# Giving a four-row mask matmul all 128 rows of the array

One small matmul of a fused kernel adds a mask. Its two operands used four partitions; after the change they use all 128, with zeros in the added rows of one of them. Nothing else is altered.

## Chip, cores and metric

The kernel runs on one core of a Trainium2 chip. The metric is device time in microseconds of one execution; a profiled execution also gives the span from the first to the last instruction, which is about 1.7 us shorter. TensorE, VectorE, ScalarE, GpSimd and SyncE are written PE, DVE, ACT, POOL and SP in the profile, and PEld is TensorE's weight load. Each run is called fast or slow by its time; only fast runs are compared.

## The reference, cut to what matters

Attention with chunk selection over 4 batches, 8 heads, 768 positions and 64 channels, followed by a gated MLP. For each query an upper bound is formed for each of 24 chunks of keys, chunks later than the query's own are masked, and the best six are attended to:

```python
ub = np.sum(np.maximum(q[:, :, :, None, :] * k_min[:, :, None, :, :],
                       q[:, :, :, None, :] * k_max[:, :, None, :, :]), axis=-1)
causal = pos[:, None] // chunk >= np.arange(nc)[None, :]
ub = np.where(causal, ub, -1000000000.0)
top_chunks = np.argsort(ub, axis=-1)[..., -top_k:]
# ... masked softmax of q k^T over the chosen chunks, times v ...
# ... then relu(x @ w_in), a norm, a spatial matmul, a gate, and @ w_out ...
```

## The kernel before

Heads are worked on in 16 pairs. Per pair the bounds of the query tiles 1 to 5 (128 queries each) are made in one PSUM bank: two matmuls for the bound itself and one that adds the chunk mask. The mask has rank four, because a tile of 128 queries holds four chunks: `sub_chunk` says to which of the four a query belongs, `later` which chunks are later than that one.

```python
P = 128; CHUNK = 32                       # CPT = P // CHUNK = 4, NCH = 24
sub_chunk = cp.tile([CPT, P], F16)
later = cp.tile([CPT, 2, 2 * NCH - CPT], F16)
# ... set once at the start, from the identity and by a select on GpSimd ...

def bounds(self):
    ub = self.ub = ps_tr.tile([P, 512], F32, tag="tr", name="ub")
    for qi in range(1, NQT):
        for m in range(2):                                     # L220
            mm(ub[:, (qi - 1) * W:qi * W], lhsT=self.rq[:, m, qi * P:(qi + 1) * P],
               rhs=self.km[:, m].rearrange("p h c -> p (h c)"), start=(m == 0), stop=False)
        mm(ub[:, (qi - 1) * W:qi * W], lhsT=sub_chunk,         # L222
           rhs=later[:, :, NCH - CPT * (qi + 1):2 * NCH - CPT * (qi + 1)],
           start=False, stop=True)
```

So there are 16 groups of five units, and a unit is bound, bound, mask: 80 mask matmuls of 48 columns. Around them stand the score matmuls, exponentials on ScalarE, value matmuls and, from about 59 us on, the MLP of the batch before. Loads of q, k, v and of the MLP's weights are issued from GpSimd. A scheduler orders each engine's instructions when the program is built.

The softmax here doesn't subtract the row's maximum and nothing guards it: scores larger than these inputs give would overflow.

Of the kernel before, what the change touches and what calls it, by code (L numbers as in the profile page):

```python
# [11 lines left out]
F16 = mybir.dt.float16  # L12
# [4 lines left out]
P = 128  # L17
CHUNK = 32
# [30 lines left out]
def kernel(  # L49
# [13 lines left out]
    NCH = S // CHUNK  # L63
# [8 lines left out]
    CPT = P // CHUNK  # L72
# [3 lines left out]
    cp = ctx.enter_context(tc.tile_pool(name="const", bufs=1))  # L76
# [29 lines left out]
    kh_ring = [[ring.tile([P, S], F16, name=f"kh{i}_{hi}") for hi in range(2)] for i in range(NB)]  # L106
    identity = cp.tile([P, P], F16)
    tri = cp.tile([P, P], F16)
    sub_chunk = cp.tile([CPT, P], F16)
    later = cp.tile([CPT, 2, 2 * NCH - CPT], F16)  # L110
    expand = cp.tile([D, S], F16)
    eps_t = cp.tile([P, 1], F32)

# [16 lines left out]
    def init_expand():  # L130

        nc.vector.tensor_scalar(expand.rearrange("d (c s) -> d c s", s=CHUNK),
                                in0=identity[0:D, 0:NCH].unsqueeze(2).to_broadcast([D, NCH, CHUNK]),
                                scalar1=NEG, scalar2=None, op0=Alu.mult)
        nc.vector.tensor_copy(sub_chunk.rearrange("d (c s) -> d c s", s=CHUNK),
                              identity[0:CPT, 0:CPT].unsqueeze(2).to_broadcast([CPT, CPT, CHUNK]))

    def init_masks():

# [315 lines left out]
    at(B0, init_ring, 0)  # L455
    at(B0, init_small)
    at(B0, init_expand)
    at(B0, init_masks)
    at(B0, load_k, 0, 0, 1)
# [105 lines left out]
```

## Time and profile before

| | before |
|---|---|
| time, median (4 runs) | 234.35 us (233.95 to 236.59) |
| span of the profiled run, mean granted clock | 231.2 us, 0.999 |
| unit of two bounds and a mask, start to start | 277 ns |
| group of five units, to the next matmul | about 1.38 us |

The first part of the page gives each engine's busy time, its share of the span and its instructions:

```profile
PE 207.5 (90%) x2022; PEld 126.8 (55%) x2022; DVE 154.1 (67%) x453; ACT 164.6 (71%) x335; POOL 79.9 (35%) x99
```

TensorE is the busiest. The table by windows says where; its columns are the window, then busy time and instruction count for TensorE, its weight loads, VectorE, ScalarE and GpSimd, then clock, DMA share and GB/s:

```profile
60.00:90.00 30.00, 27.99 (x293) 17.92 (x292) 26.51 (x73) 23.49 (x50) 16.20 (x17) 1.00 2.24 141
90.00:120.00 30.00, 29.40 (x283) 17.25 (x281) 23.60 (x73) 23.40 (x51) 7.94 (x8) 1.00 1.29 147
120.00:150.00 30.00, 29.45 (x294) 17.86 (x293) 21.67 (x62) 24.45 (x51) 5.87 (x6) 1.00 0.44 60
```

From 60 us on it is TensorE's program that sets the pace. Before that the chain of waits (the chain that ended last), cut to 20 to 62 us, by line, reads:

```profile
by line: ACT e L263 35.0%; PE ub L220 8.9%; PE ub L222 7.4%; PE sc L258 7.1%; issue 5.9%; PE acc L281 5.3%; POOL vt_81 L335 3.4%; PE trm L244 2.4%; PE kTp L169 2.4%; ACT km_86 L188 2.2%; POOL e L270 2.1%; ACT a_413 L249 1.9%; ACT a_543 L249
```

Exponentials lead there, and the bounds and masks (`ub`) follow with 16%.

Now the mask itself. The groups of instructions, split by shape, list the mask's matmul, the bounds' matmul and both weight loads (busy us, mean ns of one, idle before):

```profile
L222 PE MATMUL ub<-later,sub_chunk 4*128 4x48 f16 x80 | 15.4, 193 | 0.0
L220 PE MATMUL ub<-km_86,rq 128*128 128x48 f16 x80 | 9.3, 192 | 2.1 <-ACT km_86 L188 0.7 <-DVE rq L209 0.6 <-ACT rq L211 0.5
L220 PEld LDWEIGHTS <-rq 128*128 128x128 f16 x160 | 10.4, 97 | 7.3 <-issue 2.1 <-DVE rq L209 0.8 <-ACT rq L211 0.6
L222 PEld LDWEIGHTS <-sub_chunk 4*128 4x128 f16 x80 | 7.3, 91 | 3.3
```

By the means a mask costs the same as a bound, about 190 ns. That is a trap: the duration of a matmul says little here of how soon the next one starts (65-column value matmuls of 193 ns each start 31 ns apart, below). The spacing is in the timeline of TensorE (start us, us from the first start to the last end of the row, line, tile, count):

```profile
33.31 0.44 PE L281 MATMUL acc<-vt_80,e 128*128 128x65 f16 x9
33.59 0.18 PE L220 MATMUL ub<-km_87,rq 128*128 128x48 f16 x1
33.70 0.19 PE L222 MATMUL ub<-later,sub_chunk 4*128 4x48 f16 x1
33.83 0.22 PE L220 MATMUL ub<-km_87,rq 128*128 128x48 f16 x2
33.98 0.19 PE L222 MATMUL ub<-later,sub_chunk 4*128 4x48 f16 x1
34.10 0.22 PE L220 MATMUL ub<-km_87,rq 128*128 128x48 f16 x2
34.26 0.19 PE L222 MATMUL ub<-later,sub_chunk 4*128 4x48 f16 x1
...
34.81 0.19 PE L222 MATMUL ub<-later,sub_chunk 4*128 4x48 f16 x1
34.93 0.23 PE L169 MATMUL kTp<-identity,k 128*128 128x128 f16 x1
```

Masks start every 0.277 us. Single records show that a mask starts 115 ns after the bound ahead of it and the next matmul 124 ns after the mask, while two bounds stand 25 to 40 ns apart. Nine 65-column value matmuls fit into 0.44 us: less the duration of the last, 0.19 us, that leaves eight steps of 31 ns.

### The profile page before, as it was taken

The page shows a single profiled execution, that of the slowest core. Times are in us where ns is not written, and L with a number is a line of the kernel's source. Part 1 is how long each engine was busy: PE and PEld are TensorE (multiplying, and loading weights), DVE is VectorE, ACT ScalarE, POOL GpSimd, SP SyncE. Part 2 cuts the span into 40 slices and gives each one's busy share as a digit, 9 for nine tenths or more (in the row PEclk, how much of TensorE's full clock was granted, in tenths as well). Part 3 has the DMA queues.
Part 4 walks back from the last instruction along what each step waited for, and adds up shares of the span by engine and source line. Part 5 has one row for each costly group of instructions (what it writes and reads, how often), then busy time and mean ns, then how long its engine had stood idle before and what let it go on. Part 6 is the DMA issues. An engine that isn't in the chain of part 4 may idle for free.

```text
span 231.2 us, 5296 instructions
## 1 busy us (share of the span) xinstructions
PE 207.5 (90%) x2022; PEld 126.8 (55%) x2022; DVE 154.1 (67%) x453; ACT 164.6 (71%) x335; POOL 79.9 (35%) x99
## 2 busy tenths in 40 slices
PE   0279999898799989999999999999999999999990
PEld 0166677575466656556555555665555655544430
DVE  5347887787869899987567957573477355276610
ACT  2416797798778887679798976688898976476033
POOL 7991879860975153117011131111111111100000
PEclk9999999999999999999999999999999999999999
DMA  7999999999999999949991096427220325530376
GB/s 42 188 154 150 142 157 150 192 157 156 171 146 153 128 110 147 133 82 137 205 197 34 3 62 88 78 48 173 110 54 12 31 52 102 168 129 0 68 112 231
DMA packets 111273, 26.89 MB, mean 116 GB/s; under 512 B 105872, under 2 KB 107664, under 8 KB 111248
## 3 DMA queue, kind: packets, MB, share of 16 engines
q0 software_dynamic: 76512, 12.19, 84.8%
q1 hardware_dynamic: 34736, 14.36, 31.6%
q8 instruction: 16, 0.26, 0.5%
q14 instruction: 9, 0.07, 0.1%
HBM read 24.38 MB, written 6.29 MB: 133 GB/s over the span
## 4 chain that ended last, share of the span: by engine, by line
PE 60%; ACT 13%; DVE 9%; DMA 7%; POOL 6%; issue 3%; SPq 1%; ACTq 0%; POOLq 0%; DVEq 0%
PE mlp L380 30%; PE sc L258 9%; ACT e L263 8%; PE acc L281 6%; PE ub L220 4%; PE ub L222 4%; DMA k<-in_k_dram 3%; DVE vn L404 3%; DMA xT<-x_1868 3%; PE tr L244 2%; POOL qs_83 L330 2%; ACT o L429 1%; PE tr L204 1%; POOL k L321 1%; DVE kmm L177 1%
## 5 line engine op out<-in xcount | busy, mean ns | idle before, releaser
L263 ACT ACTIVATE e<-sc 128x512 f16<-128x512 f32 x192 | 97.9, 554 | 20.9 <-PE sc L258 17.7
L380 PE MATMUL mlp<-w_in_sb,xT 128*128 128x512 f16 x192 | 51.9, 379 | 0.5 <-DMA xT<-x_1868 0.5
L270 POOL TENSOR_SCALAR_AFFINE_SELECT e<-e 128x768 f16<-128x768 f16 x24 | 21.2, 883 | 89.1 <-ACT e L263 89.0
L281 PEld LDWEIGHTS <-e 128*128 128x128 f16 x672 | 30.8, 97 | 16.2 <-POOL e L270 2.0
L380 PE MATMUL mlp<-vn,wsT 128*128 128x512 f16 x144 | 39.1, 379 | 0.0
L419 DVE SCALAR_TENSOR_TENSOR g<-mlp,b_col,u 128x512 f16<-128x512 f32 x24 | 18.0, 748 | 13.3 <-PE mlp L380 12.0
L380 PE MATMUL mlp<-w_out_sb,gT 128*128 128x512 f16 x96 | 26.3, 379 | 0.1
L429 ACT COPY o<-mlp 128x512 f32<-128x512 f32 x24 | 14.2, 590 | 15.3 <-PE mlp L380 11.5
L380 PEld LDWEIGHTS <-xT 128*128 128x128 f16 x192 | 17.0, 98 | 14.5 <-DMA xT<-x_1868 1.0
L392 DVE BATCH_NORM_STATS2 stats<-vraw 128x6 f32<-128x512 f32 x24 | 16.6, 690 | 8.3 <-ACT vraw L390 8.1
L380 PEld LDWEIGHTS <-wsT 128*128 128x128 f16 x144 | 12.9, 98 | 10.2
L390 ACT ACTIVATE vraw<-mlp 128x512 f32<-128x512 f32 x24 | 14.4, 600 | 5.1 <-PE mlp L380 5.1
L412 ACT ACTIVATE u<-mlp 128x512 f16<-128x512 f32 x24 | 14.5, 605 | 2.6 <-PE mlp L380 2.5
L319 POOL DMA_DIRECT2D k<-in_k_dram x14 | 14.5, 1052 | 4.9 <-DMA k<-in_k_dram 2.3
L222 PE MATMUL ub<-later,sub_chunk 4*128 4x48 f16 x80 | 15.4, 193 | 0.0
L220 PEld LDWEIGHTS <-rq 128*128 128x128 f16 x160 | 10.4, 97 | 7.3 <-issue 2.1
L281 PE MATMUL acc<-vt_80,e 128*128 128x65 f16 x252 | 13.8, 193 | 0.5 <-DVE x_1440 L289 0.5
L404 DVE TENSOR_SCALAR vn<-vraw,mv,rstd 128x512 f16<-128x512 f32 x24 | 12.9, 596 | 0.6 <-ACT rstd L402 0.6
L380 PEld LDWEIGHTS <-gT 128*128 128x128 f16 x96 | 8.6, 98 | 7.8 <-DMA gT<-g 1.1
L281 PE MATMUL acc<-vt_81,e 128*128 128x65 f16 x252 | 12.8, 193 | 0.0
L288 DVE RECIPROCAL rec<-acc 128x6 f32<-128x6 f32 x32 | 6.0, 187 | 8.2 <-PE acc L281 8.0
L220 PE MATMUL ub<-km_86,rq 128*128 128x48 f16 x80 | 9.3, 192 | 2.1 <-ACT km_86 L188 0.7
(225 smaller groups left out, 387.3 us busy)
## 6 DMA issues: line engine op xcount, KB each, us to landing
out_dram<-o SPq DMA_DIRECT2D x24, 256.0 KB, 2.3
k<-in_k_dram POOLq DMA_DIRECT2D x14, 192.0 KB, 11.3
vt_80<-in_v_dram POOLq DMA_DIRECT2D x3, 384.0 KB, 9.2
qs_84<-in_q_dram POOLq DMA_DIRECT2D x6, 192.0 KB, 8.9
vt_81<-in_v_dram POOLq DMA_DIRECT2D x3, 384.0 KB, 10.6
ws_raw<-in_moe_w_spatial_dram POOLq DMA_DIRECT2D x6, 192.0 KB, 8.1
w_in_sb<-in_moe_w_in_dram POOLq DMA_DIRECT2D x8, 128.0 KB, 5.3
qs_85<-in_q_dram POOLq DMA_DIRECT2D x4, 192.0 KB, 8.5
```

Of the source, the lines that this page charges most:

```text
L220: mm(ub[:, (qi - 1) * W:qi * W], lhsT=self.rq[:, m, qi * P:(qi + 1) * P], rhs=self.km[:, m].rearrange("p h c -> p (h c)"), start=(m == 0), ...
L222: mm(ub[:, (qi - 1) * W:qi * W], lhsT=sub_chunk, rhs=later[:, :, NCH - CPT * (qi + 1):2 * NCH - CPT * (qi + 1)], start=False, stop=True)
L258: mm(sc[:, col:col + n], lhsT=self.kh[hi][:, t * P:(t + 1) * P], rhs=self.a[hi][:, q0:q0 + n], start=True, stop=not diag)
L263: nc.scalar.activation(out=self.e[hi][:, g * 512:g * 512 + width], in_=sc[:, 0:width], func=Act.Exp, scale=scale)
L270: nc.gpsimd.affine_select(out=blk, in_=blk, compare_op=Alu.is_ge, fill=0.0, base=0, channel_multiplier=-1, pattern=[[0, NQT], [1, P]])
L281: mm(self.av[:, qi, :], lhsT=self.e[hi][:, c:c + P], rhs=self.v[hi][:, t, 0:D + 1], start=first and n == 0, stop=last and n == len(blocks) ...
L319: nc.gpsimd.dma_start(out=t[:, :, :, 1 - hi, :].rearrange("p x t d -> p (x t) d"), in_=source(k, b, h, 2))
L380: mm(st[group][:, 0:cols], lhsT=lhsT, rhs=rhs, start=(j == 0), stop=(j == n - 1))
L392: nc.vector.bn_stats(stats, st["vraw"][:, ti, :])
L404: nc.vector.tensor_scalar(st["vn"][:, ti, :], in0=st["vraw"][:, ti, :], scalar1=st["mv"][:, ti, 0:1], scalar2=st["rstd"][:, ti, :], op0=Al ...
L419: nc.vector.scalar_tensor_tensor(g, in0=vs, scalar=b_col[:, ti:ti + 1], in1=st["u"][:, ti, :], op0=Alu.add, op1=Alu.mult)
L429: nc.scalar.copy(o_sb, o_ps)
```

## The change

The intent is that the mask runs in the same form of the array as everything around it. In the built program a four-row operand gets an array tile of 32 rows by 128 columns; a 128-row operand gets 128 by 128, as all other matmuls have.

```diff
-    sub_chunk = cp.tile([CPT, P], F16)
-    later = cp.tile([CPT, 2, 2 * NCH - CPT], F16)
+    sub_chunk = cp.tile([P, P], F16)
+    later = cp.tile([P, 2, 2 * NCH - CPT], F16)
 ...
         nc.vector.tensor_copy(sub_chunk.rearrange("d (c s) -> d c s", s=CHUNK),
-                              identity[0:CPT, 0:CPT].unsqueeze(2).to_broadcast([CPT, CPT, CHUNK]))
+                              identity[:, 0:CPT].unsqueeze(2).to_broadcast([P, CPT, CHUNK]))
```

The first four columns of the identity are zero below row 3, so the added rows of `sub_chunk` are zero; those of `later` hold finite values that meet these zeros. The order of instructions on every engine is the same before and after.

## The prediction

> **What bounds the kernel now.** Mean clock 0.999 (cores view). TensorE is busy 207.5 of 231.2 us (engine table); by windows, 28.0 of 30 us from 60 to 90, 29.4 from 90 to 120, 29.5 from 120 to 150, with VectorE and ScalarE at 22 to 27. From 20 to 60 us it is busy 36.4 of 40 by modelled ends, but the chain of waits passes through ScalarE (exponentials), the mask groups and VectorE in turn. Until 19.6 us the chain is loads of k; from 180 us dense 512-column matmuls.
>
> **What the change does to an instruction.** The built program gives the four-row mask operands an array tile of 32 rows; all other matmuls have 128. Start to start in the timeline, in 15 of 16 groups of five: bound to mask 115 ns, mask to next matmul 124 ns. A unit of two bounds and a mask takes 277 ns. Full-row neighbours are much closer: bound to bound 25 to 40 ns, the 65-column value matmuls about 31 ns. The mask's weight load takes 90 ns against 95 for full rows, its matmul 191 against 182 to 196: row count is not the cost, the two transitions are. [...] With full rows every operand has the same tile[...]: I estimate 85 to 105 ns a unit. The mask matmul's own duration will hardly change; its spacing will.
>
> **Sum.** 80 masks x (277 - 95) ns = about 14.5 us less TensorE time. Nothing moves: the order on TensorE, ScalarE and the DMA queues is the same. Added: the setup copy of sub_chunk on 128 partitions for 4 (0.51 us, same elements a row) and the fill and select of `later` on GpSimd (0.16 and 0.26 us, same elements a row). I expect the same within 0.1 us.
>
> **How much is on the critical path.**
> - First group (11.7 us): 0.9 us shorter, but the chain there is the load of k landing at 19.6 us. Worth 0.
> - Five groups from 20 to 60 us: 4.5 us shorter, all on the chain, but ScalarE is busy 33 of 40 us, so part turns into waits for exponentials. Worth about 2 us.
> - Ten groups from 60 to 176 us: 9 us shorter, TensorE-bound. VectorE (26.5 of 30 us from 60 to 90) and ScalarE come nearer to the limit. Worth about 6.5 us.
> - After 180 us: 0.
>
> Together 8.5 us: **226.1 us**, range 222.8 to 229.9. Faster by over 2%: 0.9; within 2%: 0.09; slower by over 2%: 0.01.
>
> **What will show it right or wrong.**
> - Timeline: bound to mask and mask to next 25 to 45 ns; five units in about 0.5 us instead of 1.39. Above 100 ns, the tile of 32 rows was not the cause.
> - Groups: mask loads and matmuls 128*128, mean near 95 and 185 ns. TensorE's busy sum falls by 8 to 14 us.
> - Chain of waits: mask and bound lines fall from 8% together to 2 or 3%; exponentials and VectorE gain. TensorE's waits for ScalarE and VectorE grow by several us, mostly from 20 to 60 us.
> - The tail from 180 us on keeps its length.
>
> **What would make it wrong.** Full-row masks may be slow for another reason (the two-piece access of `later`, 24 columns twice): the gain halves. The freed time may be lost to ScalarE and VectorE from 60 us on (gain 4 to 5 us). Or shorter mask groups may relieve the chain entirely (gain 12 us).

80 x (277 - 95) ns is about 14.5 us, of which 0 + 2 + 6.5 + 0 = 8.5 us were put on the critical path. The 95 ns is the estimate, the middle of 85 to 105 ns; three starts at the 25 to 40 ns measured between bounds make 75 to 120 ns.

## The result, and the profile after

| | before | after |
|---|---|---|
| time, median (4 runs each) | 234.35 us | 224.72 us (223.5 to 225.59) |
| ratio of fast runs | | 0.957 (95% interval 0.948 to 0.965) |
| span, clock of the profiled run | 231.2 us, 0.999 | 221.8 us, 0.989 |
| unit of two bounds and a mask | 277 ns | 75 ns |

A ratio is the mean time of one kernel's fast runs over that of the other's fast runs of the same rounds, so not quite the ratio of the medians, which are over all runs of a kernel.

Busy times of the page, and the three windows, in the same columns:

```profile
PE 194.7 (88%) x2022; PEld 118.6 (53%) x2022; DVE 153.0 (69%) x453; ACT 163.8 (74%) x335; POOL 80.3 (36%) x99
```

```profile
60.00:90.00 30.00, 28.15 (x326) 17.85 (x327) 27.88 (x85) 24.62 (x54) 16.31 (x17) 1.00 2.24 147
90.00:120.00 30.00, 28.30 (x292) 16.48 (x289) 23.82 (x67) 25.03 (x52) 7.86 (x8) 1.00 1.12 147
120.00:150.00 30.00, 29.68 (x329) 18.07 (x328) 22.60 (x72) 26.13 (x57) 6.28 (x7) 1.00 0.50 62
```

TensorE is still busy nearly all the time from 60 us on, but starts more instructions in each window (x326 for x293 in the first): the same program runs through it faster. TensorE's busy sum fell by 12.8 us (207.5 to 194.7), the span by 9.4, so its idle time grew by 3.4 us.

The timeline of the same group as above:

```profile
31.85 0.59 PE L281 MATMUL acc<-vt_80,e 128*128 128x65 f16 x14
32.28 0.18 PE L220 MATMUL ub<-km_87,rq 128*128 128x48 f16 x1
32.30 0.18 PE L222 MATMUL ub<-later,sub_chunk 128*128 128x48 f16 x1
32.33 0.21 PE L220 MATMUL ub<-km_87,rq 128*128 128x48 f16 x2
32.38 0.18 PE L222 MATMUL ub<-later,sub_chunk 128*128 128x48 f16 x1
...
32.60 0.18 PE L222 MATMUL ub<-later,sub_chunk 128*128 128x48 f16 x1
32.63 0.49 PE L169 MATMUL kTp<-identity,k 128*128 128x128 f16 x6
```

From the first mask's start to the fifth's it is 0.30 us for 1.11 us. Each of the three starts of a unit is now 25 ns from the next (about 40 ns in the two groups before 22.3 us, where the records of full clock begin). The groups by shape show the same matmul with almost the same duration (187 for 193 ns), as a busy time of 8.2 for 15.4 us only because busy time doesn't count overlap twice:

```profile
L222 PE MATMUL ub<-later,sub_chunk 128*128 128x48 f16 x80 | 8.2, 187 | 0.0
L222 PEld LDWEIGHTS <-sub_chunk 128*128 128x128 f16 x80 | 6.8, 99 | 0.0
```

The chain of waits from 20 to 62 us, by line:

```profile
by line: DMA kT<-k 23.4%; DMA k<-in_k_dram 17.4%; PE sc L258 5.9%; PE acc L281 5.2%; issue 5.2%; DVE kmm L177 4.3%; POOL vt_82 L335 3.5%; POOL vt_81 L335 3.4%; DVE kmm L181 2.6%; PE mlp L380 2.6%; PE tr L244 2.3%; DVE max_283 L232 2.2%; POO
```

Bounds and masks are nearly gone from it, but so are most exponentials. Loads and transposing copies of k have taken their place, which the prediction had not foreseen. Over the whole span the pieces of this chain on bounds and masks sum to 18.6 us before and 3.1 us after, those on DMA to 16.6 and 39.2 us. The chain that ends last differs between executions: in the traces of the two repeats of the changed kernel, exponentials keep 8.4 us of the chain between 20 and 62 us (14.7 us before). What all three share is DMA, 15.6 to 17.2 us in this stretch, where before had none.

Since the order is the same, the same matmul can be looked up in both traces. The 400th starts at 46.53 us before and 43.20 us after (3.33 us won), the 600th at 65.02 and 62.99 us (2.03 us), the 1800th at 188.97 and 179.79 us (9.18 us). So the gain shrinks by 1.3 us between 43 and 63 us, although two more groups in this stretch free about 1 us each, and it grows by 7.1 us after that.

### The profile page after: what moved, and what is told of

Its sections match the earlier page's. It is cut to its first block, busy times and chain, and to the rows that moved or that the text cites. A ratio compares the mean times of both kernels' runs of the same rounds, so it can differ in the third digit from the quotient of the medians.

```text
span 221.8 us, 5296 instructions
## 1 busy us (share of the span) xinstructions
PE 194.7 (88%) x2022; PEld 118.6 (53%) x2022; DVE 153.0 (69%) x453; ACT 163.8 (74%) x335; POOL 80.3 (36%) x99
## 4 chain that ended last, share of the span: by engine, by line
PE 44%; DMA 18%; DVE 17%; ACT 9%; POOL 7%; issue 3%; POOLq 0%; ACTq 0%; DVEq 0%; SPq 0%
PE mlp L380 27%; PE sc L258 7%; DMA k<-in_k_dram 7%; PE acc L281 5%; DMA kT<-k 4%; ACT e L263 4%; DMA gT<-g 3%; DVE kmm L177 3%; DMA xT<-x_1868 3%; DVE kmm L181 2%; ACT o L429 2%; PE tr L244 2%; POOL qs_83 L330 2%; DVE vn L404 1%; POOL k L321 1%
## 5 line engine op out<-in xcount | busy, mean ns | idle before, releaser
L419 DVE SCALAR_TENSOR_TENSOR g<-mlp,b_col,u 128x512 f16<-128x512 f32 x24 | 17.9, 748 | 12.8 <-PE mlp L380 11.5
L429 ACT COPY o<-mlp 128x512 f32<-128x512 f32 x24 | 14.1, 590 | 14.2 <-PE mlp L380 10.5
L392 DVE BATCH_NORM_STATS2 stats<-vraw 128x6 f32<-128x512 f32 x24 | 16.6, 691 | 8.2 <-ACT vraw L390 8.1
L380 PEld LDWEIGHTS <-wsT 128*128 128x128 f16 x144 | 12.9, 97 | 10.1
L319 POOL DMA_DIRECT2D k<-in_k_dram x14 | 14.5, 1051 | 4.2 <-DMA kT<-k 1.7
L261 PE MATMUL sc<-tri,identity 128*128 128x128 f16 x48 | 11.1, 232 | 0.0
L220 PEld LDWEIGHTS <-rq 128*128 128x128 f16 x160 | 8.4, 99 | 5.1 <-issue 2.1
L177 DVE TENSOR_REDUCE kmm<-kT 128x24 f16<-128x768 f16 x10 | 9.4, 941 | 2.2 <-DMA kT<-k 2.2
```

The lines of the kernel that those rows point to most:

```text
L177: nc.vector.tensor_reduce(self.kmm[:, 0, :], self.kT.rearrange("d (c ch) -> d c ch", ch=CHUNK), axis=AX.X, op=Alu.max)
L319: nc.gpsimd.dma_start(out=t[:, :, :, 1 - hi, :].rearrange("p x t d -> p (x t) d"), in_=source(k, b, h, 2))
L380: mm(st[group][:, 0:cols], lhsT=lhsT, rhs=rhs, start=(j == 0), stop=(j == n - 1))
L392: nc.vector.bn_stats(stats, st["vraw"][:, ti, :])
L419: nc.vector.scalar_tensor_tensor(g, in0=vs, scalar=b_col[:, ti:ti + 1], in1=st["u"][:, ti, :], op0=Alu.add, op1=Alu.mult)
L429: nc.scalar.copy(o_sb, o_ps)
```

## The experiments

### Is it rows, or the form of the array? 64 and 68 rows

The diff is the same for both, with R = 64 or R = 68. In the built program 64 rows get an array tile of 64 by 128 and 68 rows one of 128 by 128. The order on TensorE is that of before. Both results are correct.

```diff
-    sub_chunk = cp.tile([CPT, P], F16)
-    later = cp.tile([CPT, 2, 2 * NCH - CPT], F16)
+    sub_chunk = cp.tile([R, P], F16)
+    later = cp.tile([R, 2, 2 * NCH - CPT], F16)
-                              identity[0:CPT, 0:CPT].unsqueeze(2).to_broadcast([CPT, CPT, CHUNK]))
+                              identity[0:R, 0:CPT].unsqueeze(2).to_broadcast([R, CPT, CHUNK]))
```

> 64 rows instead of 4 in both operands of the mask; the built program gives them an array tile of 64 rows. Theory [...]: nothing is gained, because 64 is still not the 128 of the neighbours: bound to mask about 115 ns, mask to next about 124 ns, 234.5 us, ratio 1.00 +- 0.01. Rival (the cost falls with the share of rows filled): a gain between none and the whole, about 5 us. Correct result.

> 68 rows, 60 short of full; the built program gives them an array tile of 128 rows. Theory (tile, not rows): the whole gain comes, gaps of 25 to 40 ns, 224.7 us, ratio 0.957 +- 0.01, as with 128 rows. Rival (all rows must be filled): gaps above 100 ns and no gain, or about half the gain. Correct result.

Timeline of TensorE with 64 rows:

```profile
26.03 0.19 PE L222 MATMUL ub<-later,sub_chunk 64*128 64x48 f16 x1
26.16 0.22 PE L220 MATMUL ub<-km,rq 128*128 128x48 f16 x2
26.31 0.19 PE L222 MATMUL ub<-later,sub_chunk 64*128 64x48 f16 x1
```

and with 68 rows:

```profile
25.62 0.18 PE L222 MATMUL ub<-later,sub_chunk 68*128 68x48 f16 x1
25.64 0.21 PE L220 MATMUL ub<-km,rq 128*128 128x48 f16 x2
25.70 0.18 PE L222 MATMUL ub<-later,sub_chunk 68*128 68x48 f16 x1
```

With 64 rows the gaps are 115 and 126 ns and a unit takes 280 ns: 234.62 us, ratio 1.007 (1.002 to 1.011), no gain at all. With four rows more the gaps are 25 ns, a unit 75 ns: 224.53 us, ratio 0.961 (0.956 to 0.966), the whole gain. The cost doesn't follow the share of rows filled; it jumps where the tile changes from 64 to 128 rows. To fill all rows, as the change does, is not needed.

### Is a four-row matmul slow in itself? Masks together

The five masks of a group are moved behind its ten bounds, with four rows and with 128. Only the first matmul of the bank now has `start=True`. The order on the other engines stays the same (compared on a copy with 128 rows and unshifted line numbers).

```diff
             for qi in range(1, NQT):
                 for m in range(2):
-                    mm(..., lhsT=self.rq[...], rhs=self.km[...], start=(m == 0), stop=False)
-                mm(..., lhsT=sub_chunk, rhs=later[...], start=False, stop=True)
+                    mm(..., lhsT=self.rq[...], rhs=self.km[...], start=(qi == 1 and m == 0), stop=False)
+            for qi in range(1, NQT):
+                mm(..., lhsT=sub_chunk, rhs=later[...], start=False, stop=(qi == NQT - 1))
```

> Four rows as before, but the five masks of a group stand together after the ten bounds, so a group changes the tile twice instead of ten times. Theory ([...]a mask by itself costs nothing special): mask to mask 25 to 40 ns, one gap of 115 and one of 124 ns left; a group falls from 1385 to about 570 ns, eight tenths of the gain: 227 us, ratio 0.965. Rival (every four-row matmul or its weight load is slow in itself, for example because the load isn't pulled ahead): mask to mask stays at 115 to 124 ns, a group about 900 ns or more, at most half of the gain: 230 us or more. Correct result.

> The same order with all 128 rows: the control for the order. Theory: no tile change is left to save, so as the changed kernel, 224.7 us, ratio 0.957 +- 0.006; gaps 25 to 40 ns. Rival (the order itself helps or hurts): differs by over 1.5 us. Correct result.

The timeline with four rows shows one group:

```profile
25.55 0.41 PE L220 MATMUL ub<-km,rq 128*128 128x48 f16 x10
25.89 0.29 PE L223 MATMUL ub<-later,sub_chunk 4*128 4x48 f16 x5
26.12 0.51 PE L245 MATMUL trm<-identity,qs 128*128 128x128 f16 x6
```

Five four-row masks take 0.29 us from the first start to the last end; single records put them 25 to 40 ns apart, as close as full-row ones. Only the way in (115 ns) and the way out (110 ns) remain. Time: 226.23 us, ratio 0.970 (0.965 to 0.974), which by the medians is 7.1 of the 8.8 us that full rows gain in the same call, the eight tenths expected. With 128 rows in this order: 224.56 us, ratio 0.962 (0.958 to 0.966), the same as the change. So a four-row matmul among its like is not slow here; the change of the tile between two matmuls is, and it can also be made rarer by ordering.

### Which stage gives the gain? Full rows early or late only

Both use 128-row tiles, of which some pairs read four rows only. Pairs 0 to 5 have their groups before 60 us. The order is that of before on all engines.

```diff
+            R = P if self.i < 6 else CPT          # late_full: self.i >= 6
             ub = self.ub = ps_tr.tile([P, 512], F32, tag="tr", name="ub")
 ...
-                mm(..., lhsT=sub_chunk, rhs=later[:, :, ...], start=False, stop=True)
+                mm(..., lhsT=sub_chunk[0:R], rhs=later[0:R, :, ...], start=False, stop=True)
```

> The changed kernel again, to compare with the others of this call on the same chip: 224.7 us, ratio 0.957.

> Full rows only for the masks of head pairs 0 to 5 (groups before 60 us), four rows for the other ten. Prediction as recorded: the early groups are worth 2 us, so 232.4 us, ratio 0.991. Rival read from the trace after: 3.3 us won by 43 us, then 1.3 us of it lost to a stretch of half clock from 53.0 to 56.4 us; with the half clock 232.4, without it 231 us, ratio 0.985.

> Full rows only for pairs 6 to 15 (groups from 60 us on), four rows for the first six. Prediction as recorded: worth 6.5 us, 228 us, ratio 0.972. If freed TensorE time were lost to VectorE and ScalarE: 230 us. From the traces (matmul 600 to 1800): 7.2 us, 227.2 us, ratio 0.969. No half clock before 60 us is expected here, since TensorE is as busy there as before.

Measured against 233.66 us for before: all pairs 224.07 us (ratio 0.960), early pairs 231.59 us (0.993, interval 0.988 to 0.998), late pairs 226.24 us (0.969, 0.964 to 0.974). By the medians 2.1 us come from the early six groups and 7.4 us from the late ten; their sum, 9.5, is the whole gain of 9.6. The one early run with nearly full clock (0.999) took 230.63 us, 2.1 us less than such runs of before (232.7 us), so the early gain is no larger without half clock, as far as one run can tell. Half clock appears in both traces, from 54.1 to 57.5 us in the early run and, not before 60 us as expected, from 63.7 to 67.1 us in the late one.

### What takes part of the gain? The half clock

The trace after has the clock at half (0.50) from 53.0 to 56.4 us; the trace of before has none there. A run that added TensorE work in that stretch was to bring the clock back:

```diff
+                if self.i == 4:
+                    mm(sc[:, col:col + n], lhsT=self.kh[hi][:, t * P:(t + 1) * P],
+                       rhs=self.a[hi][:, q0:q0 + n], start=True, stop=True)
                 mm(sc[:, col:col + n], lhsT=self.kh[hi][:, t * P:(t + 1) * P],
                    rhs=self.a[hi][:, q0:q0 + n], start=True, stop=not diag)
```

> Full rows, and each score matmul of head pair 4 is issued twice (the same values written twice; 2 us of TensorE work added between 44 and 56 us, where TensorE waits for others). Theory: the half clock from 53.0 to 56.4 us in the trace after comes from too little TensorE work in this stretch and costs about 1.3 us: the mean clock goes back to 0.998 and the time falls to 223.5 us, ratio 0.951. Rival (the half clock costs nothing as TensorE waits there anyway, or doesn't depend on this work): same or slower, 224.7 to 226 us. Correct result.

It failed: 235.89 us median, four of the six runs slow, a ratio of 0.996 (0.989 to 1.003) for the two fast ones, and the profiled run among the slow (half clock from 62.5 to 65.9 and from 69.4 to 76.2 us). The scheduler had answered the added matmuls with another order on all engines. In its trace VectorE waited 9.4 us for a transposing copy of k, and TensorE then 5.2 us for VectorE:

```profile
DVE kmm L177 <- DMA kT<-k: 11.1, 2, 9.4
PE acc L284 <- DVE x L292: 7.6, 4, 5.2
```

So it tells nothing of the clock. What can be said comes from all runs. Of 31 fast runs of the kernel before in the experiments, 8 had a mean clock of 0.997 or more and took 232.7 us on average; the other 23 took 233.6 us. So runs with a lower mean clock took about 1 us longer, and they occur with both kernels. Of the 16 runs of the changed kernel, all fast, none had 0.997, and the mean clock was 0.9889 for 0.9914. That may be chance (one fast run with full rows and four buffers of k had 1.0), and no run here tested whether full rows make half clock more frequent.

The kept traces do show what comes before it. Every stretch of half clock up to 205 us lasts 3.41 us or twice that. If each of the 14 traces is cut into steps of this length, in line with its own stretches, and each matmul is counted with its columns at 2.4 per ns, an estimate from the traces (512-column matmuls start 216 ns apart, 128-column ones 55: 384 columns in about 160 ns), then all 19 steps with at most 1.24 us of columns are followed by half clock, and of the about 750 steps above 1.24 us one is (1.254 us). In the trace after, 22 matmuls started in the 3.413 us before the clock fell at 53.02 us, and the longest idle time was 1.16 us; their columns come to 1.21 us. So in these traces sparse TensorE work went before half clock; this is read from them, not tested by an experiment.

### What takes part of the gain? The loads

In the chain after, loads have taken the place of exponentials before 62 us. Where the early gain goes shows in the timeline of TensorE, at the last value matmuls of a head, before and after:

```profile
61.62 0.36 PE L281 MATMUL acc<-vt_82,e 128*128 128x65 f16 x6 [1.39 <-POOL e L270]
60.60 0.36 PE L281 MATMUL acc<-vt_82,e 128*128 128x65 f16 x6 [2.18 <-POOL e L270]
```

They wait for the causal select on GpSimd in both kernels, so here only 1.0 us is left of the 3.3. In the traces of `rows68`, of the first repeat (`full_again`) and of the run with four buffers of k (below), whose masks also have the full tile, the clock is full from 24 to 59 us and 2.7 to 3.0 us are still won at the 560th matmul (about 56.5 us); after this wait, of 2.9 to 3.1 us, 1.1 to 1.4 us are left. So the early gain shrinks here without half clock too.

The timeline of GpSimd shows why the select doesn't come sooner. Before:

```profile
42.80 1.43 POOL L335 DMA_DIRECT2D vt_80<-in_v_dram  x1 [0.34 <-issue]
59.22 1.43 POOL L335 DMA_DIRECT2D vt_81<-in_v_dram  x1
60.71 0.86 POOL L270 TENSOR_SCALAR_AFFINE_SELECT e<-e 128x768 f16<-128x768 f16 x1
```

After:

```profile
42.82 1.42 POOL L335 DMA_DIRECT2D vt_80<-in_v_dram  x1 [0.25 <-issue]
58.21 1.42 POOL L335 DMA_DIRECT2D vt_81<-in_v_dram  x1
59.68 0.86 POOL L270 TENSOR_SCALAR_AFFINE_SELECT e<-e 128x768 f16<-128x768 f16 x1
```

TensorE is 3 us ahead at 43 us, but the load of v is issued at the same moment, because GpSimd's issues of loads ahead of it wait for earlier loads to land (0.7 to 0.9 us each for loads of v, k and q between 38 and 43 us in the trace after; then 4.2 us for that v load, in both traces). The next v load comes only 1.0 us sooner, and the causal select of the values (`e`) stands behind it on GpSimd. Two experiments tried to change that. One moves the loads of two MLP weights later, with four rows and with full rows; these two have the same order on all engines. The other gives the tiles of k a fourth buffer.

```diff
-        at(36 + 4 * j, load_w_spatial, j)              # later_four, later_full
+        at(48 + 4 * j, load_w_spatial, j)
-        at(62 + 6 * j, load_w_out, j)
+        at(82 + 2 * j, load_w_out, j)
-        at(5 * BEATS + 2 * so, prep_w_spatial, so)
+        at(5 * BEATS + 8 + 2 * so, prep_w_spatial, so)
```

```diff
-            tiles["k", g] = sb.tile([P, 2, NQT, 2, D], F16, tag="k", name="k", bufs=3)
+            tiles["k", g] = sb.tile([P, 2, NQT, 2, D], F16, tag="k", name="k", bufs=4)  # k_four_buffers
```

> The changed kernel once more, for the chip of this call: 224.3 us, ratio 0.960.

> The kernel before (four-row masks) with the loads of w_spatial and w_out 12 to 20 beats later, out of the way of the k, q and v loads before 60 us. Theory (until 60 us the queue of loads sets the pace, so most freed TensorE time of that stage is lost): with four rows the stage is bound partly by TensorE and partly by the loads, so 0 to 3 us faster than before, 231 to 234 us. It is needed to compare with the next run; the order on the engines differs somewhat from before, but is the same in both.

> The same later loads with full rows; the orders on all engines equal those of the run with four rows and later loads. Theory (loads took the early gain): the gain of full rows over four rows is larger here than the 9.5 us without the shift, 10.5 to 12 us, and the time is 220.5 to 223 us. Rival (the early gain is lost to ScalarE and VectorE, as the prediction said, or to the order): again 9.5 us or less. Matmul 600 of the trace, which starts at 63 us in the traces with full rows, should start by 61.5 us or earlier.

> Full rows, and four buffers for the tiles of k instead of three, so that a load of k waits for no transpose of an earlier one; the order on all engines is the same. Theory (the queue is saturated, so an earlier issue only queues elsewhere): within 1 us of the changed kernel, 223.5 to 225 us. Rival (loads of k are late because they wait for a buffer): 2 us or more faster, 222 us or below.

Against 233.44 us for before: the changed kernel 223.94 us (0.959), later loads with four rows 232.77 us (0.997), later loads with full rows 226.82 us (0.971, 0.965 to 0.976), four buffers of k 225.0 us (0.961). The expectation of the later loads failed. Full rows gained 6.0 us there (232.77 less 226.82), not 10.5 to 12, and the 600th matmul started at 64.3 us, not by 61.5. The rival, that ScalarE, VectorE or the order take the early gain, allowed such a result (9.5 us or less); the run excludes none of them. Among the waits of TensorE in that trace are:

```profile
PE acc L281 <- POOL e L270: 3.5, 1, 3.5
PE mlp L380 <- DMA xT<-x: 2.3, 1, 2.3
PE kTp L169 <- DMA k<-in_k_dram: 1.8, 1, 1.8
```

The v load that stood at 58.21 us in the changed kernel is issued at 58.13 us here, so the queue was not relieved where it mattered; that the weights now press on the loads after 60 us is likely, but not shown. The profiled run had three stretches of half clock, and the clock differs over all runs: a mean of 0.983 with full rows, 0.993 with four, so the 6.0 us compare unequal clocks. The fourth buffer brought nothing, so a missing buffer for k is not what holds the loads. What its expectation calls a saturated queue is in the page this: the DMA engines are busy 90% or more in every slice from 5.8 to 98 us before and from 5.5 to 94 us after. That the loads pace the stage before 60 us is thus read from this, issue times, the wait for the select and the chain, and fits the fourth buffer; no run here removed the limit and showed the gain come back. It stays open.

No run was faster than the changed kernel beyond the scatter.

## Why the prediction was right

It gave 226.1 us with a range of 222.8 to 229.9; the median is 224.72 us.

- **The cost of a change of tile.** Right. The gaps are 115 and 124 ns with a tile of 32 rows, 115 and 126 ns with 64, and 25 ns with 128, and the 64-row, 68-row and masks-together runs exclude the rivals that were named: the share of rows filled, and a four-row matmul slow in itself. What TensorE waits for in these gaps was not shown: in before, the mask's weight load starts about 110 ns after the start of the bound ahead and its matmul 4 ns later; after, it starts 1 to 2 ns after that bound and about 24 ns ahead of its matmul.
- **The cost of a full-row unit.** Somewhat too high: 85 to 105 ns expected, 75 ns measured. It is three starts at 25 ns each, the low end of the 25 to 40 ns that the prediction had read between bounds. The rival in the prediction, a cost of the two-piece access of `later`, is excluded by the same 25 ns.
- **The sum.** 80 masks at 202 ns less (277 - 75) are about 16 us, not 14.5 us; TensorE's busy sum fell by 12.8 us, within the stated 8 to 14.
- **The share on the critical path.** Right as a sum. The late ten groups free 10.1 us (50 times 202 ns) and brought 7.4 us, 73%; the prediction had 6.5 of 9 us, 72%. It laid the rest to VectorE and ScalarE. From the 600th to the 1800th matmul TensorE's waits (over 150 ns) grew by 1.62 us: 0.65 for ScalarE, 0.26 for VectorE and 0.71 for a DMA (`xT`), which it hadn't named. The early groups were put at 2 us and brought 2.1; their reason was another (next point), so that this size fits is luck. The missing 1.1 us of the prediction is mostly the too large unit.
- **What absorbs the early gain.** Wrong in the mechanism. The prediction had exponentials and VectorE gain share in the chain, and waits of TensorE for ScalarE and VectorE grow by several us. Exponentials fell in the chain from 17.9 to 8.8 us. TensorE's waits for exponentials fell from 1.1 to 0.6 us, those for all of ScalarE went from 3.1 to 3.3 us and for VectorE from 3.4 to 4.7 us. What cut the early gain to 1.0 us was the wait for the select on GpSimd (1.39 us before, 2.18 us after), behind loads of k and v. It stood in the trace of before already, and the prediction had not counted it.
- **Set-up.** Right. The copy of `sub_chunk` takes 0.51 us in both; GpSimd's fill and select went from 0.16 and 0.26 to 0.20 and 0.28 us.
- **The tail.** Right: the last run of 40 matmuls of `w_in` starts 27.4 us before the end in before and 27.2 us after.

## What to carry to other kernels

A matmul over 4 or 64 rows in the midst of full-row ones cost two changes of the array's form here, about 200 ns together, though its own duration looked ordinary (193 ns with four rows, 187 with 128); look at the distance between starts, not at durations. Give such an operand more rows with zeros in the rest, until its array tile is that of its neighbours (68 were enough here, 64 were not), or put the small matmuls next to one another. Then count on the saving mainly where TensorE's own program sets the pace: here 73% of it arrived in such a stage, and about 2 us of some 5 us before 60 us, where TensorE runs into a wait for GpSimd that ended only 1.0 us sooner. Look for such waits in the trace of the kernel before.
